# Copies of the identity moved from GpSimd to VectorE in an attention and feed-forward kernel, with a new order of all engines

## The chip, the cores and the metric

The kernel runs on one core of a Trainium2 chip. The time is device microseconds of one execution, and smaller is better. A core has a matrix engine (TensorE, PE in the profile), three engines for elementwise work (VectorE or DVE, ScalarE or ACT, GpSimd or POOL), a queue engine (SyncE or SP) and 16 DMA engines. Each engine takes its instructions in the order in which the program gives them, and an instruction that has to wait holds up everything behind it on its engine.

## The reference, cut to what matters

Attention with a decay over the keys, for 8 batches of 8 heads, 576 tokens and 64 columns a head, and behind it a feed-forward layer whose hidden values are the product of two projections:

```python
scores = scale * np.matmul(q, k.transpose(0, 1, 3, 2))
log_f = np.log(np.clip(f, 0.0001, 1.0))
cum = np.cumsum(log_f, axis=-1)
decay = cum[:, :, :, None] - cum[:, :, None, :]
scores = np.where(causal, -1000000000.0, scores + decay)
attn = softmax(scores)                       # over the keys
x = np.matmul(attn, v)                       # (8, 8, 576, 64), then as 4608 x 512
out = ((x @ w_a) * (x @ w_b)) @ w_out        # 512 -> 1536 -> 512
```

## The kernel before

**Tiles.** Two heads are worked on together as a pair (t = 0 to 31, four pairs per batch), one head on each half of the 128 partitions. The queries of a pair are cut into row blocks i = 0 to 4 of 128 (the last of 64), and a row block needs the keys up to itself. All matmuls take fp16 and add up in fp32.

**The stages of a pair.** q and k are loaded, made fp16 (by the DMA itself in batch 0, by POOL later: `cast_qk`), transposed on PE (`pe_transpose`, L359) and copied out of PSUM (`pe_evict`, L287 to L293). PE makes the scores (`qk_group`, L551). In batch 0 PE also adds the decay, by multiplying a row of cumulative sums (`crow`) with a one-hot column taken from `pick`, and the causal mask, by multiplying `low` with `neg64`. DVE takes the maximum (L646, later fused with the decay in L674), ACT the exponential with its sum (L705), DVE the reciprocal (L713 and L715), and POOL or ACT multiplies (`do_norm`: L726 on POOL, L724 on ACT). The result is transposed, on PE for the first pairs and by a DMA transpose later (PTA and PTB), multiplied with v (L769, L784), and copied into `xT`.

**The feed-forward layer** goes over 11 blocks of 256 to 512 tokens. Each has matmuls with w_a (`psa`) and with w_b (`psb`), all under L74, a copy on ACT, a product on DVE (L1073), matmuls with w_out (`pso`), a copy and a store. The first psa needs rows 0 to 255 of all four pairs of batch 0.

**The order.** The program is a table of 2353 steps (`Op`), each with a function that issues its instructions, an engine or a choice of engines, and the steps that it needs. Two strings that a planner wrote fix the rest: `ORDER` is one sequence of all steps, and each engine works through its own of them in that sequence; `CHOICE` has one letter for each step that may run on more than one engine (A for ACT, D for DVE, P for POOL, S for SP). `SLOTS` says which buffer of a ring each step takes. At the places where PE has nothing to do, 24 steps `wake` multiply the identity with itself, and nothing reads the result.

**The steps around the change.** `ident` (step 2, on POOL) writes the 128x128 identity `ident16`: a memset and a select. `pick` (step 3, L86 to L90) clears two tiles `pickh` and copies each of the four 32x32 diagonal blocks of the identity into `pick` and into one of `pickh`: two memsets and eight copies. `const` (step 4, L93 to L102, on POOL) makes `neg64` and two tiles `low`: three memsets and six selects. `flo` (L233) makes the low halves of `crow`, `clip` (L225), the logarithm (L260) and the scan (L228) its sums. The planner's table has 1.2 us for ident, 1.0 (DVE) or 2.1 (POOL) for pick and 2.2 for const. `CHOICE` sends pick to POOL.

```python
def picks(e):
    for x in pickh:
        VEC[e].memset(x, 0.0)
    for m in range(4):
        x = slice(32 * m, 32 * m + 32)
        VEC[e].tensor_copy(out=pick[x, :], in_=ident16[x, x])
        VEC[e].tensor_copy(out=pickh[m // 2][x, :], in_=ident16[x, x])
```

Of the kernel before, what the change touches and what calls it, by code (L numbers as in the profile page):

```python
# [25 lines left out]
def kernel(  # L26
# [13 lines left out]
    B, H, S, D = q.shape  # L40
# [64 lines left out]
    def paddings():  # L105
# [36 lines left out]
        PA:03212031203120312031203120312031;PB:01010101010101010101010101010101;S:010101101010100101011010101101  # L142
        00010110111101010101001011010110110011100101001101010101001010010101011001010010101010;a16:0210210212012
        01201201201201201210120210212012010201201201201202120120121021021021021021012021210120121021201202012;bc
        :0210210210210210210210210210;ff:03120312013203210320302302133030201230301201203211031120120320123012031
        20132103213212302102130230230132132013201231203023013231213201302310231023102103203203201321203120312030
        23023102132132321302130213213201320312012302310230232130230210321023123102310312301301203120312031203103
        21023120320320123102310203120120123023102302130230312031203123123102301230213023121320311032032103210310
        131023101230123120312032032102130213211321321332012301312301201203203203201;ht:0dcba981234567d0bc9a81324
        567d0bc9a813542d670cb9851a324d670bc19854a32d6708cb1a9543d2670c89b1a543d06279c8b51a3460dc2;n16:0110010100  # L150
        01010010101001010101;n32:0210202102101201201012012002020102101021210210;nv:01010101;osb:0101010110101010
        01010101101101010010;qd:010101010101010101010101;sc:0101010101010101101001010110101001100101010101101001
        0101101011010101011100101101010101101010010101010101010110110110101101010101;st:054321054321054321054321
        05432105
# [91 lines left out]
    o_k = Op(None, {"DVE": 1.0, "POOL": 2.1}, picks, [o_i], prio=-300, name="pick")  # L246
# [10 lines left out]
    for lo, hi in ((0, 256), (256, S)):  # L257
# [5 lines left out]
                prio=-300, name="fscan")  # L263
# [945 lines left out]
    for n in cuts:  # L1209
# [3 lines left out]
        0 1 46 52 2 58 5 6 29-31 37 32 33 38-40 34 36 35 42 62 3 47 53 4 43 267 262 500 7 8 54 48 41 9  # L1213
        56 50 44 10 82 59 60 83 11 85 91 97 61 86 87 92 12 45 66 287 71 55 49 51 63 64 57 93 288 98 289
        99 127 94 130 136 131 132 137 138 13 290 172 14 15 128 16 291 175 181 176 183 182 177 139 133
        142 96 339 268 141 135 263 17 279 274 173 18 67 144 143 184 65 88-90 187 145 178 217 220 226 264
        188-190 265 340 19 218 221 222 227 228 232 223 266 341 229 95 72 180 186 146 74 140 179 185 73
        134 230 192 191 225 224 75 20 21 113 22 233 234 269 84 103 109 270 114 271 231 104 105 110 203
        158 23 24 342 204 25 159 205 206 100 106 248 211 249 102 108 101 129 111 107 77 280 76 112 343
        212 148-150 166 26 167 121 256 117 27 28 154 122 257 115 155 281 174 151 156 235 283 193 199 153  # L1220
# [6 lines left out]
        409 415 416 294 252 213 209 253 316 317 210 214 318 1733 1734 319 403 365 323-325 258 215 216  # L1227
        259 320 360 284 286 285 247 308 273 326 1736 254 346 375 368 410 376 369 1741 404 443 444 1737
        1738 321 255 322 1742 353 327 370 445 502 377 378 503 1739 371 398 1735 512 332 495 1743 446 328
        504 417 372 420 421 427 428 447 329 1745-1747 330 422 331 1748 1744 379 366 373 418 374 352 513  # L1230
# [10 lines left out]
        1789-1791 1793 714 653 707 632 633 1792 706 598 600 626 625 619 614 1799 441 439 1794 596 442  # L1241
        1795 1797 562 721 584 547 534 561 715 654 708 592 578 722 585 440 599 1796 601 637 1798 627 620
        638 602 639 1774 709 723 719 577 621 611 591 604 597 603 729 724 1800 656 660-662 1809 1801 1811
# [8 lines left out]
        796 760 652 784 797 783 909 811 911 855 1862 1863 695 1864 771 901-903 755 696 905 761 769 762  # L1252
        1872 1873 1865 800 801 906 907 802 803 908 816 1874 814 812 743 735 910 912 779 742 794 818 798
        819 804 832 826 825 750 856 1876-1879 833 1875 820 827 828 821 1867 839 840 1868 1869 835 834
# [119 lines left out]
```

## Time and profile before

| | |
|---|---|
| runs | 400.53, 402.37, 403.38 us; median 402.37 |
| the profiled execution | 405.31 us, span 403.6 us from its first to its last instruction |
| granted TensorE clock, mean | 0.996 |
| PE busy by stretch (0 to 14, 14 to 40, 40 to 90 us) | 8.17, 23.51, 49.74 us |
| first feed-forward matmul (psa) | 40.1 us |
| DMA | 76.87 MB, 190 GB/s mean |

In a row of the order of time, the first number is the start in us from the first instruction, the second is how long the row lasts, then engine, line, operation, `out<-in` by the names of the tiles, shapes and the count of instructions that the row merges. In square brackets stands how long the engine was idle ahead of it, and what ended that. In the table of stretches, each engine has its busy us and, in brackets, its instructions. A grouped row has the count, the busy us and the mean ns of one instruction, and then the idle time before them and who ended it.

### The profile page before, as it was taken

To read this page: it belongs to the slowest core of one execution; us is meant where nothing else is said; L and a number is where in the kernel's file an instruction comes from. 1 tells how busy PE (TensorE), PEld (TensorE's weight loads), DVE (VectorE), ACT (ScalarE), POOL (GpSimd) and SP (SyncE) were. 2 spreads that over 40 slices of the span, in tenths; PEclk is the share of its full clock that TensorE was granted. 3 is DMA by queue.
4 is the path that set the end of the run, shared out by engine and by line. 5 is a ranking of instruction groups with operands and counts; after the bars stand their busy time and mean duration, and the time that the engine had idled before them with its cause. 6 is when DMAs were issued, how large, how long until landed. Compare 5 with 4: busy or idle time off the path is not lost.

```text
span 403.6 us, 14685 instructions
## 1 busy us (share of the span) xinstructions
PE 388.4 (96%) x5768; PEld 243.5 (60%) x5768; DVE 291.5 (72%) x958; ACT 288.1 (71%) x797; POOL 261.7 (65%) x485
## 2 busy tenths in 40 slices
PE   5798999999999999999999799999999999999997
PEld 2455887978867655555565455555555555556675
DVE  5687989998877899976978667778887673234141
ACT  4688899998897778767887688887968762423231
POOL 8699694977979489849988477788776583000000
PEclk9899999999999999999999999999999999999999
DMA  7989999999999999999989999999997787100112
GB/s 124 243 173 146 170 137 169 234 240 293 224 248 284 211 316 193 225 229 263 222 247 210 270 260 231 222 269 217 229 213 171 166 164 161 54 2 10 44 54 80
DMA packets 147365, 76.87 MB, mean 190 GB/s; under 512 B 124384, under 2 KB 128352, under 8 KB 147296
## 3 DMA queue, kind: packets, MB, share of 16 engines
q1 hardware_dynamic: 132856, 68.72, 74.4%
q0 software_dynamic: 14256, 7.08, 14.5%
q8 instruction: 45, 0.74, 0.7%
q14 instruction: 24, 0.20, 0.2%
q10 hardware_dynamic: 184, 0.14, 0.1%
HBM read 52.05 MB, written 9.58 MB: 153 GB/s over the span
## 4 chain that ended last, share of the span: by engine, by line
PE 74%; DMA 8%; POOL 8%; DVE 3%; issue 3%; ACT 2%; POOLq 0%; ACTq 0%; DVEq 0%
PE psb L74 20%; PE psa L74 20%; PE pso L74 17%; DMA PTB<-PB 5%; PE sc L551 4%; PE pvx L769 3%; POOL PA L726 3%; PE psT L359 2%; PE sc L539 2%; DVE S L674 2%; DMA q<-in_q_dram 2%; PE psP L74 1%; DMA out_dram<-osb 1%; PE sc L74 1%; POOL PB L726 1%
## 5 line engine op out<-in xcount | busy, mean ns | idle before, releaser
L674 DVE CUSTOM_DVE_ANT_0 S<-sc,spread 64x576 f32<-64x576 f32 (+4 forms) x232 | 125.8, 562 | 15.6 <-PE sc L551 2.6
L74 PE MATMUL psa<-xT,wa 128*64 128x512 f16 (+2 forms) x1056 | 113.7, 341 | 0.8 <-ACT a L289 0.5
L74 PE MATMUL psb<-xT,wb 128*64 128x512 f16 (+2 forms) x1056 | 113.3, 341 | 0.2 <-DVE ht L1073 0.2
L1073 DVE TENSOR_TENSOR ht<-psb,a 128x512 f16<-128x512 f32 (+1 forms) x114 | 73.5, 657 | 42.2 <-PE psb L74 27.1
L74 PE MATMUL pso<-wout,ht 128*64 128x512 f16 x840 | 101.9, 380 | 0.0
L726 POOL TENSOR_SCALAR PA<-PA,st 128x384 f16<-128x384 f16 (+2 forms) x188 | 87.6, 478 | 15.5 <-DVE st L715 9.4
L289 ACT CAST a<-psa 128x512 f16<-128x512 f32 (+1 forms) x114 | 63.0, 557 | 44.9 <-PE psa L74 41.1
L705 ACT ACTIVATE PA<-S,st 128x256 f16<-128x256 f32 (+2 forms) x168 | 84.0, 504 | 9.8 <-DVE st L674 8.7
L726 POOL TENSOR_SCALAR PB<-PB,st 128x512 f16<-128x512 f16 (+1 forms) x89 | 62.5, 709 | 26.4 <-DVE st L715 13.9
L74 PEld LDWEIGHTS <-wb 128*64 128x64 f16 x1056 | 58.9, 110 | 32.4 <-issue 2.2
L74 PEld LDWEIGHTS <-wa 128*64 128x64 f16 x1056 | 57.8, 110 | 33.1 <-issue 4.0
L74 PEld LDWEIGHTS <-ht 128*64 128x64 f16 x912 | 48.9, 110 | 34.4 <-issue 1.4
L705 ACT ACTIVATE PB<-S,st 128x512 f16<-128x512 f32 x56 | 40.3, 721 | 3.5 <-DVE st L674 3.4
L705 ACT ACTIVATION_READ_ACCUMULATOR PA<-S,st 128x1 f32 x168 | 32.2, 192 | 0.0
L701 ACT ACTIVATE PB<-S,st 128x576 f16<-128x576 f32 x28 | 21.7, 775 | 12.1 <-POOL PA L726 3.6
L674 DVE CUSTOM_DVE_ANT_1 S<-sc,spread 128x256 f32<-128x256 f32 x48 | 19.8, 420 | 9.9 <-POOL spread L631 2.7
L631 POOL TENSOR_SCALAR_AFFINE_SELECT spread<-spread 128x768 f32<-128x768 f32 x24 | 20.8, 867 | 7.6 <-DMA spread<-cum_d 7.6
L769 PEld LDWEIGHTS <-nv 128*64 128x64 f16 x640 | 22.5, 110 | 5.4 <-issue 0.5
L293 DVE COPY osb<-pso 128x512 f32<-128x512 f32 x17 | 11.7, 690 | 16.7 <-PE pso L74 11.6
L674 DVE DVE_READ_ACCUMULATOR2_ANT st<- 128x1 f32 (+1 forms) x280 | 23.0, 82 | 0.0
L715 DVE RECIPROCAL st<-st 128x2 f32<-128x2 f32 x128 | 17.9, 155 | 6.1 <-ACT PA L705 4.1
L291 POOL TENSOR_SCALAR q<-q 128x1152 f16<-128x1152 f32 x14 | 16.1, 1153 | 9.2 <-DMA q<-in_q_dram 3.5
(107 smaller groups left out, 492.2 us busy)
## 6 DMA issues: line engine op xcount, KB each, us to landing
spread<-cum_d SPq DMA_DIRECT2D x24, 576.0 KB, 6.4
out_dram<-osb SPq DMA_DIRECT2D x35, 256.0 KB, 3.3
q<-in_q_dram SPq DMA_DIRECT2D x14, 576.0 KB, 5.4
k<-in_k_dram SPq DMA_DIRECT2D x14, 576.0 KB, 5.4
v<-in_v_dram SPq DMA_DIRECT2D x24, 256.0 KB, 5.7
wout<-in_moe_w_out_dram POOLq DMA_DIRECT2D x3, 512.0 KB, 5.9
nv<-in_v_dram POOLq DMA_DIRECT2D x8, 128.0 KB, 4.8
wa<-in_moe_w_a_dram POOLq DMA_DIRECT2D x2, 512.0 KB, 7.2
```

What stands on the lines that cost most here:

```text
L74: nc.tensor.matmul(out=out[r], lhsT=lhsT[:, r], rhs=rhs, **kw)
L289: nc.scalar.copy(out=out_, in_=in_)
L291: VEC[e].tensor_scalar(out=out_, in0=in_, scalar1=0.125, scalar2=1.0, op0=MUL, op1=MUL)
L551: nc.tensor.matmul(out=dst, lhsT=lhsT, rhs=rhs, start=start, stop=stop, skip_group_check=True)
L631: nc.gpsimd.affine_select(out=c[:, :, 0:SM].rearrange("p h (j k) -> p h j k", k=128), in_=c[:, :, SM:2 * SM].rearrange("p h (j k) -> p h j ...
L674: nc.vector.tensor_tensor_reduce(out=o, in0=x, in1=y, scale=-1.0, scalar=3e38, op0=ADD, op1=MIN, accum_out=m)
L701: nc.scalar.activation(out=p_blocks(t, 4), in_=T[("s" if direct else "z", t, 4)], func=EXP, bias=st[:, 8:9], scale=sign, accum_out=st[:, 1 ...
L705: nc.scalar.activation(out=p_blocks(t, i)[:, :, h, :], in_=(T[("s", t, i)][:, h, :] if direct else T[("z", t, i)][:, h * n:h * n + n]).rea ...
L715: nc.vector.reciprocal(out=st[:, 20 + 2 * i:22 + 2 * i], in_=st[:, 10 + 2 * i:12 + 2 * i])
L726: VEC[e].tensor_scalar(out=p, in0=p, scalar1=st[:, c:c + 1], scalar2=1.0, op0=MUL, op1=MUL)
L769: nc.tensor.matmul(out=o[HP[h], 128 * i:128 * i + 128], lhsT=vt[:, j, pr + NP * h, :], rhs=pt[:, base_blk[i] + 2 * block_at(t, i, j) + h, ...
L1073: nc.vector.tensor_tensor(out=ht[:, 0:n_], in0=T.pop(("psb", t0, fbs))[:, 0:n_], in1=T.pop(("a16", t0, fbs))[:, 0:n_], op=MUL)
```

## The change

One line of the table fixes `pick` on DVE. The three strings `ORDER`, `CHOICE` and `SLOTS` are replaced as a whole; the functions, the instructions of each step and the feed-forward blocks stay.

```diff
-    o_k = Op(None, {"DVE": 1.0, "POOL": 2.1}, picks, [o_i], prio=-300, name="pick")
+    o_k = Op("DVE", 1.0, picks, [o_i], prio=-300, name="pick")
...
     ORDER = """
-        0 1 46 52 2 58 5 6 29-31 37 32 33 38-40 34 36 35 42 62 3 47 53 4 43 267 262 500 7 8 54 48 41 9
-        56 50 44 10 82 59 60 83 11 85 91 97 61 86 87 92 12 45 66 287 71 55 49 51 63 64 57 93 288 98 289
...
+        0-2 52 46 62 58 5 6 29 3 30 31 37 32 38 33 39 34 36 40 35 42 4 47 53 43 262 500 267 7-9 48 54 10
+        44 56 50 41 82 63 83 11 85 91 65 86 87 97 64 12 49 51 55 13 59 45 57 66 67 74 88 89 287 99 98 92
...
     CHOICE = """
-        ASPDDPDADAAADDDPPPPPAPAPAAADPPPPPPPAPDADDPPPPPPPPADDDDPPPPPPAPPADAADDAAAADDADPPPPPPPAPAADAPA
+        SADDPDADDADADAPPPAPPPPPDDADAPPAPPAPPDDDDPAPAAPPPPDADDAPAPPAAAPDAAADADAAAADDDAPPPPPPPAADDAPAP
...
```

Sorted by engine, the new strings put these steps first (k0 and q1 stand for the halves of k and q of batch 0, m for a second part of a load):

| engine | before | after |
|---|---|---|
| POOL | load k0, load q0, **ident**, load k1, load q1, **pick**, load k0m, load q0m, **const**, flo, paddings, load v | **ident**, load q0, load k0, load q1, load k1, **const**, load k0m, load q0m, flo, paddings, load v |
| DVE | memsets, clip, clip, scan, scan, copy and flo of crow, maxima | memsets, **pick**, clip, clip, scan, scan, copy and flo of crow, maxima |
| ACT | logarithms, copies to qT and kT, table for the exponential | logarithms, table for the exponential, copies to qT and kT |
| PE | 4 wakes, transposes q0, k0, 2 wakes, scores of pair 0 | 5 wakes, transposes k0, q0, 1 wake, scores of pair 0 |
| SP | load f, store of sums, loads q, k of batch 1, q of batch 2 | load f, store of sums, loads k of batch 1, q of batch 2, q of batch 1 |

Of the steps with a choice, 20 normalizations go from POOL to ACT and 7 from ACT to POOL, all in pairs 0 to 7; some 60 copies out of PSUM change between ACT and DVE over the whole kernel. The matmul steps that stand ahead of the first psa are the same but for one (`ptr1A1` in place of `ptr0A1`), and all 24 wakes still stand among them.

More of the change, by code (lines that the diff above doesn't have):

```diff
@@ L147 @@
[L147 to L151, printed above, removed]
@@ L152 @@
[L152 to L154 removed]
+        PA:03212310230123012301230123012301;PB:01010101010101010101010101010101;S:010110101001011010101010101101
+        00101010100101010101001010110101010101010101101010101100101010110101001010101010101010;a16:0210210210210
+        21021021021021021201201201201201201201201201201021012012012012021021021021212021010210210210120120120;bc
@@ new lines @@
+        :0210210210210210210210210210;ff:03120312021321302312013202022000102102301321302302101231023013223013021
+        32031021321320313010312031230231023012310231031231203121320312012031230123010231203120120312031201301031
+        20310231023123102102121321012102103213021301231201302312010230130231031010310230132012301203120321032013
+        01201302310230213210310230132102103120312012120320321321023103201320132013213023102120302132032103210321
+        023012130130132130213230130132013201301301301303012301203120320320320320321;ht:0dcba981234567d0bc9a18234
@@ L155 @@
+        567d0bc89a154320d769bc8451ad203769b5c481ad203794b65ac81d2036974cb5a81d24306c97b51a83d4206;n16:0110101010
+        01101101010101010101;n32:0210101212021021021210101020212010210102121001;nv:01010101;osb:0101010101010010
+        00101101010101001010;qd:010101010101010101010101;sc:0110101010101010101010100101010101010011101100100101
+        0101010101010101010011010100100101111010101001001011011010010100101010101010;st:054321053421053421053412
+        05341205
     """
@@ new lines @@
+        44 56 50 41 82 63 83 11 85 91 65 86 87 97 64 12 49 51 55 13 59 45 57 66 67 74 88 89 287 99 98 92
+        93 61 60 263 268 127 130 136 172 288 14-16 131 138 137 132 128 289 175 181 176 142 182 177 183
+        139 178 133 184 279 274 264 17 290 291 173 18 143 144 217 179 71 140 185 135 339 180 186 203 19
+        187 220 226 188 189 100 145 190 204 218 232 147 77 221 228 227 222 340 20-22 94 229 265 341 269
[11 rows of a table added]
+        320 321 259 322 326 368 369 327 1738 260 261 370 1741-1743 216 376 1739 377 1744 446 502 398
[15 rows of a table added]
@@ new lines @@
+        642 1820 643 641 720 729 622 715 578 724 679 591 680-682 1824 1826 645 644 646 561 1804 563 585
[4 rows of a table added]
+        1847 756 757 774 758 1849 759 1850 811 651 1851 782 775 754 788 760 734 1852 789 748 1853-1855
+        781 1848 1856 1857 711 712 776 652 790 791 713 1858 772 777 783 784 693 694 1808 1859 901 695
+        1862 923 904 911 855 795 812 762 761 742 735 750 755 736 796 743 769 696 902 785 903 797 771 814
+        1863 1864 787 817 749 905 912 792 800 818 798 801-803 820 1872 826 825 819 1860 832 778 821 828
@@ new lines @@
+        1873 827 1865 816 1874 1867 1876 833 1875 815 906 839 829 840 804 907 861 806 799 856 779 813
+        780 805 831 931 763 764 1861 1868 834 1877 835 841 1878 1879 908 909 1869 1880-1882 1884 1883
[3 rows of a table added]
+        1898-1900 928 859 932 1902 940 933 946 934 1901 880 939 947 1903 1904 850 857 838 881 874 1107
[11 rows of a table added]
+        1088 1090 1091 1075 967 1964-1966 968 1963 1967 1968 1130 1970 1093 1048 1969 1134 1136 1092
[4 rows of a table added]
+        1987 1132 1120 1155 1145 1152 1196 1156 1122 1129 1160 1988-1991 1121 1161 1053 1054 1098 1097
[10 rows of a table added]
@@ new lines @@
+        2039 1340 1357 1358 2007 1315 1373 2048 2045 2049 1345 1211 1256 1327 1213 1263 1322-1324 1271
[6 rows of a table added]
+        1426 1427 1507 2073 1508 1509 1432-1434 1438 1435 2076 2077 2074 2078 2080 1422 2082 1439 1441
+        2081 2084 2086 1341 1349 1405 1467 1400 1399 1392 2079 1384 1326 1385 1445 1410 1446 2085 1447
+        1440 2083 1421 1464 1419 1462 1412 1411 1393 1386 1428 1468 2087 1475 1469 1482 2088 2090 1470
+        2089 2092 1477 2093 1471 2091 1442 1369 1531 1529 1517 1414 2075 2070 1483 1476 1478 2094-2096
[8 rows of a table added]
@@ new lines @@
+        1620 1563 1568 1570 1663 2133 1524 1579 1549 2136-2138 1527 2139 1503 1526 1608 1609 1525 1611
+        1622 1610 1626 1627 1544 1587 1504 2140 1625 1669 1664 1612 1640 1634 1633 1600 1613 1628 1636
+        1635 1629 2141 2144-2146 2148 1641 2149 1643 1637 2142 1630 2147 1666 1606 1670 2150 1671-1673
[4 rows of a table added]
+        1530 1653 1696 1654 1655 1697 1656 1650 1676 1639 1675 1659 2143 2180-2182 2184 1694 1698 1699
+        2185 2183 1700 2175 1573 1617 2186 2188 2190 2192 2193 1574 2189 2191 1657 1658 1651 1660 2187
@@ L1323 @@
+        1618 2194 2197-2199 1661 2202 2195 2200 1702 1695 1701 1689 1690 1683 1704 1703 2203 2204 2207
[4 rows of a table added]
+        2289 2268 2270-2272 2275 2276 2269 2264 2291 2273 2277 2292-2295 2278 2296 2298 2297 2299-2301
+        2274 2279 2328 2302-2308 2310 2312 2309 2314 2313 2311 2315 2316 2318 2320 2317 2321 2319
+        2322-2324 2326 2325 2327 2329-2335 2338-2340 2343-2345 2336 2337 2341 2346 2342 2347-2352
     """
     CHOICE = """
-        ASPDDPDADAAADDDPPPPPAPAPAAADPPPPPPPAPDADDPPPPPPPPADDDDPPPPPPAPPADAADDAAAADDADPPPPPPPAPAADAPA
@@ L1326 @@
-        PAPPPPPADADPPPPPPPAADADAPPPAPPPPPADAADDDADAADADAAAAAAAAAADAAADDADDDDADAADDADAAAADAAAAAAAAAAA
-        ADADDDADADADDAAAAAADDDDDAADDDDDAAADAAADAADDADAADAD
+        SADDPDADADDADAPPPAPPPPPDDADAPPAPPAPPDDDDPAPAAPPPPDADDAPAPPAAAPDAAADADAAAADDDAPPPPPPPAADDAPAP
+        APPPPPDAADPAAPPAPPPDAAAAPPAAAPPADADAAAADDADAAADAAADAAAAADADDADDADADADDAAAADAAAADDAAAADDDAAAA
+        AADDADADDAADDAADAAAADAAAADAADDAAADAADADDAAADADADD
     """
```

38 lines of the change are left out of this document (removed), and 155 rows, old and new, of the table ORDER.

## The prediction

> **What bounds the kernel now.** I read the page first, then five stretches of the span, then the chain of waits of the first 41 us, then the first 16 us in order of time.
>
> ```profile
> span 403.6 us, 14685 instructions
> ...
> PE 388.4 (96%) x5768; PEld 243.5 (60%) x5768; DVE 291.5 (72%) x958; ACT 288.1 (71%) x797; POOL 261.7 (65%) x485
> ```
> ```profile
> core 0: us, PE busy (x) PEld busy (x) DVE busy (x) ACT busy (x) POOL busy (x), PEclk, DMA share, GB/s
> 0.00:14.00 14.00, 8.17 (x128) 4.00 (x128) 7.88 (x16) 6.93 (x15) 12.12 (x41) 1.00 0.86 174
> 14.00:40.00 26.00, 23.51 (x436) 14.29 (x436) 19.55 (x45) 21.28 (x66) 22.02 (x40) 0.93 0.94 170
> 40.00:90.00 50.00, 49.74 (x1040) 40.58 (x1036) 46.44 (x162) 48.22 (x132) 37.30 (x61) 1.00 1.21 193
> 90.00:345.00 255.00, 251.23 (x3568) 150.55 (x3566) 200.95 (x710) 195.56 (x556) 190.24 (x345) 1.00 1.02 228
> ```
> PE is busy 49.74 of the 50 us from 40 to 90 and 251.23 of the 255 after that, so from 40 to 345 us it stands still for 0.26 + 3.77 us in all. The first 40 us are different: their 8.17 + 23.51 busy us hold the 24 `wake` steps, which compute nothing. So the start of the first feed-forward matmul (psa) is the mark to watch. If it comes earlier, a nearly full PE moves with it. The chain of waits says who is late ahead of the mark (columns: start, us, what):
>
> ```profile
> 8.17 6.31 DMA q<-in_q_dram
> ...
> 20.92 0.02 POOL PA L726
> ...
> 28.89 0.59 POOL wb L510
> 29.48 0.04 issue
> 29.52 2.85 POOL PA L726 x6
> ...
> 40.15 0.88 PE psa L74 x13
> ```
> First comes a load that POOL issued at 8.17 and that landed at 14.48; later POOL itself, from 20.92 to 32.4, with normalizations (L726), casts and the issues of weight loads. Now the start, first POOL's rows alone, then those of the other engines:
>
> ```profile
> 1.33 0.81 POOL L334 DMA_DIRECT2D k<-in_k_dram  x1 [0.81 <-POOLq L1358]
> ...
> 2.73 0.22 POOL masks.py:197 MEMSET ident<- 128x128 f16 x1
> 3.03 0.29 POOL masks.py:199 TENSOR_SCALAR_AFFINE_SELECT ident<-ident 128x128 f16<-128x128 f16 x1
> ...
> 4.72 0.21 POOL L86 MEMSET pick<- 128x32 f16 x2
> ...
> 6.20 0.79 POOL L89 COPY pick<-ident 32x32 f16<-32x32 f16 x1
> ...
> 7.37 0.27 POOL L90 COPY pick<-ident 32x32 f16<-32x32 f16 x1
> 7.58 0.60 POOL L334 DMA_DIRECT2D k<-in_k_dram  x1
> 8.17 0.60 POOL L334 DMA_DIRECT2D q<-in_q_dram  x1
> 8.81 0.15 POOL L93 MEMSET neg<- 128x64 f16 x1
> ...
> 10.28 0.54 POOL L102 TENSOR_SCALAR_AFFINE_SELECT low<-low 64x128 f16<-64x128 f16 x2
> ```
> ```profile
> 3.37 3.34 PE L74 MATMUL wake<-ident 128*64 128x512 f16 x16 [3.37 <-POOL ident masks.py:199]
> ...
> 4.42 0.70 DVE L225 TENSOR_SCALAR cum_f<-cum_f 96x256 f32<-96x256 f32 x2 [2.16 <-DMA cum_f<-in_f_dram]
> ...
> 4.87 0.78 ACT L260 ACTIVATE cum_l<-cum_f 96x256 f32<-96x256 f32 x2 [1.25 <-DVE cum_f L225]
> ...
> 5.32 1.67 DVE L228 TENSOR_TENSOR_SCAN cum_f<-cum_f,cum_l 96x256 f32<-96x256 f16 x2 [0.21 <-ACT cum_l L260]
> ...
> 7.16 0.65 ACT L287 ACTIVATE qT<-psT 128x576 f16<-128x576 f16 x1 [1.51 <-PE psT L359]
> ...
> 8.36 1.28 ACT L221 ACT_TABLE_LOAD   x1
> ...
> 8.55 0.34 PE L551 MATMUL sc<-crow,pick 64*128 64x256 f16 x4
> ...
> 10.63 0.51 PE L551 MATMUL sc<-neg,low 64*128 64x64 f16 x7 [0.59 <-POOL low L102]
> ...
> 11.17 1.96 DVE L646 TENSOR_REDUCE st<-sc 128x2 f32<-128x512 f32 x3 [2.21 <-PE sc L551]
> ...
> 14.53 0.47 PE L359 MATMUL psT<-ident,q 64*64 64x64 f16 x18 [1.41 <-DMA q<-in_q_dram]
> ...
> 16.14 0.34 PE L551 MATMUL sc<-kT,qT 64*128 64x256 f16 x4
> ```
> pick holds POOL from 4.72 to 7.64, 2.92 us for two memsets and eight copies. Behind it stand two loads and the mask constants, which end at 10.82. The first scores have their decay from `pick` by 8.89 and then wait for the masks (low); the last mask matmuls end at 11.14, and DVE's first maximum follows at 11.17.
>
> **The change, part by part.**
>
> *pick on DVE.* In the new list it stands behind DVE's first memsets and ahead of the clip of f, where DVE is idle for 2.16 us (row of 4.42). No row shows such a copy on DVE; I bound it by two small instructions of that engine:
>
> ```profile
> 0.88 0.06 DVE L216 MEMSET warm<- 128x1 f32 x1 [0.88 <-PEq L1358]
> ```
> ```profile
> 16.78 0.17 DVE L715 RECIPROCAL st<-st 128x2 f32<-128x2 f32 x1
> ```
> Ten of them are 0.6 to 1.7 us; the ends stay, and I take 1.0, nearer to the memset, because two of the ten are memsets and the copies are 32 elements wide. The idle time covers all of it, provided `ident` is there in time, so it costs nothing. Without that cover (ident at 3.32, as now) the clip would come at 4.3 to 5.0 instead of 4.42, up to 0.6 late, and all that hangs on the scan with it.
>
> *POOL's new start.* ident (2.73 to 3.32: 0.59) now goes first: 1.33 to 1.92. Four loads of batch 0 follow; two of them took 1.33 to 2.73 and two 3.32 to 4.72, 2.8 together, so they end at 4.7. Then the constants (8.81 to 10.82: 2.0) to 6.7, and then the two loads of 7.58 and 8.17, now at 6.7 and 7.3. One thing speaks against: a pick copy took 0.79 us where the last took 0.27, and it ended at 6.99 just as DVE's two scans did (5.32 + 1.67). Now the constants lie beside the scans. If their six selects are held as that copy was, twice (once for each scan), they lose 2 × 0.52 = 1.0 us: 7.7 and 8.3. So the second load gains between 0.9 us and minus 0.1. I take 0.6, nearer to the unhindered end, because the memsets of the constants come first. The Trainium skill, page "SBUF — State Buffer", section "Who interferes with whom", gives a reason for that row: a DVE instruction with two SBUF inputs contends with a GpSimd instruction that reads SBUF, though not with one that only writes. The row agrees with it; the sum by the rule in full would use the minus 0.1.
>
> The first loads of q and k are issued up to 0.6 us later, behind ident. Their transposes now wait behind wakes (3.37 + 3.34 = 6.71); the wakes start 1.4 us earlier. The cost is between nothing and 0.6; I take nothing, as ACT sets the next step: it loads its exponential table ahead of qT in the new list, from 5.65 (4.87 + 0.78) for 1.28 and a short instruction, until about 7.1, and qT began at 7.16.
>
> *First scores.* The masks are ready at 6.7 to 7.7, before the scores. The mask matmuls follow those of pick directly: 8.9 + about 0.3 = 9.2 instead of 11.14. DVE's first maximum gains 1.9 us.
>
> *Pair 1.* The second load lands 0.6 earlier, at 13.9; transposes (0.47) and a copy (0.75 on DVE now) give its scores at 15.2 instead of 16.14: 0.9, with 0.2 to 1.2 as ends.
>
> ```profile
> 16.00 0.75 DVE L291 TENSOR_SCALAR qT<-psT 128x576 f16<-128x576 f16 x1
> ```
> *Normalizations from POOL to ACT.* Counted along the two lists, 20 of them go to ACT and 7 come back, all of batches 0 and 1: 13 net, 6 by the trace's 40 us and 7 in the stretch to 90.
>
> ```profile
> L726 POOL TENSOR_SCALAR PA<-PA,st 128x256 f16<-128x256 f16 (+2 forms) x44 | 20.6, 478 | 11.1 <-DVE st L715 9.4 <-ACT PB L705 1.3
> ```
> At 0.48 us each POOL loses 2.9 us of work ahead of the mark and 3.4 after it. POOL's stretch from 20.92 to 32.4, which is the chain today, shrinks by about 2.9. What is late next is DVE: 19.55 busy us in the 26 from 14 on, and it gets three evictions more (3 × 0.75), with the last copy of batch 0 into xT behind them all. For psa I take a gain of 2.3: its ends are pair 1's 0.9, if DVE holds all that follows, and 2.9 + 0.6 = 3.5, if POOL stays the chain; it lies nearer to POOL, which the chain names. So psa starts at 37.8 instead of 40.1.
>
> *From 40 to 90 us* ACT is busy 48.22 of 50 and gets 7 × 0.48 = 3.4 us more. Its idle 1.8 doesn't hold that; 1.6 is left over, against a stage that starts 2.3 earlier. I take a loss of 0.5, with 0 and 1.6 as ends.
>
> *After 90 us* evictions swap between ACT and DVE (23 go to ACT, 20 to DVE), and the changes between shapes of matmul on PE stay (212 in the old list, 211 in the new). No row gives this a sign: I cost it at nothing. What hides it is PE's full queue; if that cover is gone at the transfers, which the new order meets elsewhere, the price is that of the 3.77 us above once more: between a gain of half of it (1.9) and a loss of all of it (3.8).
>
> **The sum.** −2.3 + 0.5 = −1.8 us. The profiled execution's own 405.31 (its span 403.6 and 1.7 around it) becomes 403.5, with a span of 401.8. It was 2.9 above the median of the runs shown (402.37, of 400.53 to 403.38), so I set the 1.8 against that median: 400.6.
>
> **The rivals.**
> 1. *The gain is hidden.* Batch 0 is through earlier, but the rows of batch 1 come no sooner, because DVE and ACT are 93% and 96% busy from 40 to 90 and can't use the earlier start; PE then runs out of batch 0 and waits. For it: those shares. Against it: POOL, not these two, is the chain before the mark. Time: 402.4, between 401.5 and 404.
> 2. *Slower: ACT becomes the bound of 14 to 90.* It does 21.28 + 48.22 = 69.5 us of work in those 76, 91%; 13 × 0.48 = 6.2 more makes 75.7. Started 1.9 earlier it has 78, so it must be 97% full to be done at 90 as now: above that share the change gains, below it loses. At 91% it needs 82.8 and ends 4.8 late: 402.37 + 4.8 = 407.2. For it: no stretch before shows ACT above 96%. Against it: part of ACT's idle time before 40 is waiting for maxima, which come earlier.
> 3. *More goes than the start.* psa gains 3.1, and half of the 3.77 us goes too: 402.37 − 3.1 − 1.9 = 397.4. For it: those waits are few and large. Against it: nothing in the diff aims at them.
> 4. *The copies on DVE hold up POOL's issues.* They now lie beside POOL's first loads. If they stop the writing of descriptors, the first q and k come later by pick's 0.6 to 1.7, past what the wakes and ACT's table cover, and the gain at the first scores falls to some 0.8: about 401.8. For it: the copy of 0.79 shows that DVE can hold POOL. Against it: issues beside DVE memsets took no longer than 0.81. The Trainium skill, the same page, section "SBUF: two separate sides", describes this as a trap for DMAs from the GpSimd queue beside DVE copies in its faster modes; no row of before shows it.
>
> **How the numbers follow.** A measurement of this kernel tells a change of about 1% from none: the bounds are 398.35 and 406.39. The forecast (398.4 to 402.0) has 0.42, rival 1 0.22, rival 2 0.17, rival 3 0.12, rival 4 0.07. Faster by over 1%: rival 3 and a little of the forecast's edge, 0.15. Slower by over 1%: most of rival 2, 0.13, and 0.03 for the loss of 3.8 after 90 on top of rival 1: 0.16. Within 1%: 0.69. The range runs from rival 3's 397.4 towards rival 2's 407.2, drawn in a little at each end so that two in ten stay out: 397.8 to 406.5.
>
> **What would show it.** Right: POOL starts with ident at 1.3; pick on DVE is over before f lands; the first mask matmuls wait for nothing; DVE's first maximum comes at about 9.3; the two loads of pair 1 are issued at 6.7 to 8.3; psa starts at about 37.8; PE stays above 49 of 50 us from 40 to 90 with ACT at 49 or more. Wrong: the clip later than 4.5, or the load of pair 1 landing after 14.5, breaks the start; PE idle for over 1 us between 38 and 90 behind ACT breaks the step from 40 to 90; new waits of PE for DMA transposes after 90 break what I put at nothing.

## The result and the profile after

The change makes no difference that can be measured. The kernel after takes 402.64 us (median of 22 runs, 400.14 to 404.81), the kernel before 402.86 us (22 runs beside it, 400.53 to 409.12); the ratio is 1.000, 95% interval 0.9978 to 1.0023. Here and below a ratio pairs a kernel with the kernel before on the same chip and leaves disturbed runs out, so it need not be the quotient of two medians. The profiled execution of after took 402.58 us with a span of 400.8 us. That of before (405.31) was 2.45 us above its median, so the two spans by themselves say too much.

The stretches of the kernel after, in the columns used for before:

```profile
core 0: us, PE busy (x) PEld busy (x) DVE busy (x) ACT busy (x) POOL busy (x), PEclk, DMA share, GB/s
0.00:14.00 14.00, 8.87 (x146) 4.45 (x146) 9.54 (x26) 8.54 (x21) 12.76 (x34) 1.00 0.84 174
14.00:40.00 26.00, 23.21 (x406) 14.14 (x404) 19.86 (x44) 18.59 (x62) 16.47 (x29) 0.87 0.95 168
40.00:90.00 50.00, 49.88 (x1042) 40.58 (x1036) 45.53 (x155) 48.88 (x135) 35.60 (x56) 1.00 1.16 187
90.00:345.00 255.00, 254.82 (x3611) 152.44 (x3607) 200.46 (x715) 201.06 (x568) 190.01 (x345) 1.00 1.01 230
```
POOL has lost a quarter of its work from 14 to 40 us (16.47 busy us, 22.02 before). But ACT and DVE have not filled up there (18.59 and 19.86), and the granted clock of PE is 0.87 where it was 0.93. Something comes later than planned. The order of time of the kernel after shows it; these rows answer to those of the start before:

```profile
2.31 0.07 DVE L86 MEMSET pick<- 128x16 uint32 x1
...
3.32 0.35 DVE L90 COPY pick<-ident 32x32 f16<-32x32 f16 x1
...
3.92 0.94 DVE L225 TENSOR_SCALAR cum_f<-cum_f 96x256 f32<-96x256 f32 x2 [0.26 <-DMA cum_f<-in_f_dram]
...
4.36 0.21 POOL L93 MEMSET neg<- 128x64 f16 x1
...
5.16 0.92 POOL L102 TENSOR_SCALAR_AFFINE_SELECT low<-low 64x128 f16<-64x128 f16 x2
...
6.15 0.65 POOL L97 TENSOR_SCALAR_AFFINE_SELECT neg<-neg 64x64 f16<-64x64 f16 x1
...
6.75 0.81 POOL L102 TENSOR_SCALAR_AFFINE_SELECT low<-low 64x128 f16<-64x128 f16 x2
...
7.07 0.65 ACT L287 ACTIVATE qT<-psT 128x576 f16<-128x576 f16 x1 [0.18 <-PE psT L359]
...
8.11 0.60 POOL L334 DMA_DIRECT2D q<-in_q_dram  x1
...
8.96 2.04 DVE L646 TENSOR_REDUCE st<-sc 128x2 f32<-128x512 f32 x3 [0.26 <-PE sc L551]
...
13.59 0.47 PE L359 MATMUL psT<-ident,k 64*64 64x64 f16 x18 [2.59 <-DMA k<-in_k_dram]
...
16.20 0.69 PE L359 MATMUL psT<-ident,q 64*64 64x64 f16 x18 [2.15 <-DMA q<-in_q_dram]
16.82 1.07 PE L74 MATMUL wake<-ident 128*64 128x512 f16 x4
...
18.44 0.50 PE L551 MATMUL sc<-kT,qT 64*128 64x256 f16 x4
```
The first half of the plan is there: pick ends on DVE at 3.67, before f lands, and DVE's first maximum comes at 8.96 instead of 11.17. Then PE waits twice for the loads of pair 1, 2.59 and 2.15 us, and the scores of pair 1 begin at 18.44 instead of 16.14. The chain of waits of the kernel after goes through the same load, and to the same mark as before:

```profile
8.11 8.05 DMA q<-in_q_dram
...
41.20 0.99 PE psa L74 x16
```
(The chain's row of psa starts 0.07 us behind the first psa matmul, which is the mark in the text and the tables.) A second profile of the kernel before (run e0 below) shows how far one profile can be trusted. Its chain of waits:

```profile
8.66 7.49 DMA q<-in_q_dram
...
42.22 1.00 PE psa L74 x16
```
The same program had the load at 16.14 (14.48 in the first profile) and psa at 42.15 (40.08). A second profile of after (e10) had the load at 15.72 and psa at 40.28 (16.16 and 41.13). So psa came on average 0.4 us earlier (40.7 against 41.1), where 2.3 were forecast. With 2.1 us between two profiles of one program this is no measurement of the difference; it agrees with the medians.

### The profile page after: what moved, and what is told of

It is laid out like the page before. It is cut to its first block, busy times and chain, and to the rows that moved or that the text cites. A ratio compares the mean times of both kernels' runs of the same rounds, so it can differ in the third digit from the quotient of the medians.

```text
span 400.8 us, 14675 instructions
## 1 busy us (share of the span) xinstructions
PE 389.7 (97%) x5768; PEld 249.9 (62%) x5768; DVE 293.1 (73%) x968; ACT 291.5 (73%) x810; POOL 254.9 (64%) x462
## 4 chain that ended last, share of the span: by engine, by line
PE 91%; DVE 3%; DMA 3%; ACT 2%; POOL 1%; issue 0%; DVEq 0%; ACTq 0%
PE psb L74 23%; PE psa L74 23%; PE pso L74 22%; PE sc L551 5%; PE pvx L769 3%; PE psT L359 2%; PE sc L539 2%; DMA q<-in_q_dram 2%; PE psP L74 2%; PE wake L74 2%; PE sc L74 2%; PE pv L769 1%; PE pvx L784 1%; DVE S L674 1%; DMA cum_f<-in_f_dram 1%; ACT PA L705 1%
## 5 line engine op out<-in xcount | busy, mean ns | idle before, releaser
L1073 DVE TENSOR_TENSOR ht<-psb,a 128x512 f16<-128x512 f32 (+1 forms) x114 | 74.4, 658 | 53.7 <-PE psb L74 42.3
L726 POOL TENSOR_SCALAR PA<-PA,st 128x128 f16<-128x128 f16 (+2 forms) x173 | 81.0, 478 | 20.8 <-DVE st L715 16.9
L726 POOL TENSOR_SCALAR PB<-PB,st 128x512 f16<-128x512 f16 (+1 forms) x91 | 63.8, 707 | 27.3 <-DVE st L715 13.4
L74 PEld LDWEIGHTS <-wa 128*64 128x64 f16 x1056 | 60.7, 110 | 30.1 <-issue 1.8
L74 PEld LDWEIGHTS <-wb 128*64 128x64 f16 x1056 | 60.4, 110 | 29.9 <-issue 1.8
L74 PEld LDWEIGHTS <-ht 128*64 128x64 f16 x912 | 50.0, 110 | 33.3 <-issue 2.4
L769 PEld LDWEIGHTS <-nv 128*64 128x64 f16 x640 | 21.9, 110 | 4.8 <-issue 0.2
L289 ACT COPY osb<-pso 128x512 f32<-128x512 f32 x22 | 12.8, 582 | 14.3 <-PE pso L74 13.8
L701 ACT ACTIVATE PB<-S,st 128x576 f16<-128x576 f32 x28 | 21.6, 773 | 1.6 <-issue 1.1
L551 PE MATMUL sc<-kT,qT 64*128 64x512 f16 (+4 forms) x144 | 21.3, 332 | 1.0 <-ACT kT L289 0.7
L638 POOL TENSOR_SCALAR_AFFINE_SELECT spread<-spread 128x256 f32<-128x256 f32 x24 | 9.7, 404 | 19.1 <-DVE st L674 19.0
```

Source lines behind the costliest of these rows:

```text
L74: nc.tensor.matmul(out=out[r], lhsT=lhsT[:, r], rhs=rhs, **kw)
L289: nc.scalar.copy(out=out_, in_=in_)
L551: nc.tensor.matmul(out=dst, lhsT=lhsT, rhs=rhs, start=start, stop=stop, skip_group_check=True)
L638: nc.gpsimd.affine_select(out=x, in_=x, compare_op=mybir.AluOpType.is_ge, fill=NEGBIG, base=0, pattern=[[0, 2], [-1, 128]], channel_multip ...
L701: nc.scalar.activation(out=p_blocks(t, 4), in_=T[("s" if direct else "z", t, 4)], func=EXP, bias=st[:, 8:9], scale=sign, accum_out=st[:, 1 ...
L726: VEC[e].tensor_scalar(out=p, in0=p, scalar1=st[:, c:c + 1], scalar2=1.0, op0=MUL, op1=MUL)
```

## The experiments

The theory at the outset was that the whole gain hangs on one load: POOL's load of the second half of q for pair 1 (step 53, issued behind step 47). The new order puts the constants (step 4) ahead of both, they are slowed beside DVE's scans, and so the load is not issued earlier. The rivals were that SP's three loads of 576 KB (steps 262, 500, 267) take the bandwidth, that the wakes are in the way, and that the other engines in their new shares set the pace. All runs in one table (us; "landed" is step 53; "psa − scores" is from the first scores of pair 1 to psa; times of one profiled execution each, except median and ratio):

| run | issued → landed | scores of pair 1 | psa | psa − scores | median (runs) | ratio to before, 95% |
|---|---|---|---|---|---|---|
| before | 8.17 → 14.48 | 16.14 | 40.08 | 23.9 | 402.86 (22) | |
| e0 before again | 8.66 → 16.14 | 18.34 | 42.15 | 23.8 | one run, 404.72 | |
| e3 pick alone | 5.31 → 11.11 | 13.83 | 37.35 | 23.5 | 400.56 (12) | 0.9934 (0.9899–0.9969) |
| e11 e3, constants first | 8.43 → 14.68 | 16.34 | 40.17 | 23.8 | 401.99 (10) | 0.9975 (0.994–1.0011) |
| after | 8.11 → 16.16 | 18.44 | 41.13 | 22.7 | 402.64 (22) | 1.000 (0.9978–1.0023) |
| e10 after again | 8.11 → 15.72 | 18.00 | 40.28 | 22.3 | one run, 401.53 | |
| e1 loads first | 4.95 → 12.96 | 14.36 | 36.91 | 22.6 | 399.20 (6) | 0.9892 (0.9848–0.9936) |
| e2 bulk later | 8.01 → 16.44 | 18.72 | 40.64 | 21.9 | 402.57 (12) | 0.9978 (0.9945–1.001) |
| e5 both | 4.96 → 13.87 | 15.28 | 36.92 | 21.6 | 399.48 (7) | 0.9923 (0.9894–0.9951) |
| e6 constants early | 6.92 → 14.13 | 16.30 | 38.22 | 21.9 | 401.45 (10) | 0.9979 (0.9955–1.0004) |
| e9 bulk from ACT | 8.12 → 12.80 | 14.21 | 36.64 | 22.4 | 401.69 (10) | 0.9926 (0.9879–0.9972) |
| e4 pick back | 10.49 → 17.82 | 20.10 | 42.37 | 22.3 | 405.59 (7) | 1.0095 (1.0064–1.0127) |
| e7 fewer wakes | 4.96 → 14.18 | 15.59 | 37.23 | 21.6 | 400.53 (12) | 0.9944 (0.9914–0.9975) |
| e8 normalizations back | 4.95 → 12.50 | 13.90 | 42.97 | 29.1 | 408.58 (4) | 1.0152 (1.0112–1.0192) |

From psa to the end of the span the profiles show 359.5 to 362.3 us in all runs but before's first profile (363.5) and e8 (364.9), in the old order (e0 360.9, e3 359.8, e11 360.0) as in the new. So within 2.9 us the time follows psa, and the column "psa − scores" splits psa in two: when pair 1 can begin, and how long the rest of batch 0 then takes.

**Before and after again** (e0, e10): no edit.

> The kernel before, unchanged, to see in a second profile whether its first 40 us and its later waits were typical. Theory (the new order starts its first psa 1.1 us later, 41.1 against 40.1, and the profile of before happened to have more waits later): psa again at 39.5 to 40.5, and PE idle from 40 to 345 us by 1 to 3 us instead of the 4.0 of the first profile; span 399.5 to 402.5. Rival (the old order always has those waits, and the new order really removed them): PE idle by 3.5 to 4.5 us again, span 402.5 to 404.5.

> The changed kernel, unchanged, for a second profile. Expected: the load of pair 1 issued at 8.0 to 8.3 and landed at 15.5 to 17, psa at 40.5 to 42, PE idle from 40 to 345 us by 0.3 to 2; span 400 to 402.5. If psa came below 39.5, the first profile's late load would not be typical, and the account of the lost gain would fall.

Measured: the rows of the table. psa moves by 2.1 us between two executions of before and by 0.9 between two of after. e0 missed its expectation for psa (42.15 for 39.5 to 40.5) and for the span (403.0 us for at most 402.5); PE's idle time from 40 to 345 us, 1.8 us, lies inside it. A difference of 1 us in a single profile carries no verdict here.

**Loads first** (e1): the two loads of pair 1 ahead of the constants, in the new order.

```diff
-... 36 40 35 42 4 47 53 43 262 500 267 ...
+... 36 40 35 42 47 53 4 43 262 500 267 ...
```


> The changed kernel with the two loads of pair 1 (steps 47 and 53) put ahead of the mask constants on POOL. Theory (these loads, issued at 8.1 us behind constants that DVE's scans stretched, and landing at 16.2 beside SP's loads, took the start's gain back): issued at 4.4 and 5.0, landed by 11.5; the scores of pair 1 at 13 to 15 instead of 18.4; constants end at about 8.7, so the first masks wait by 0 to 0.4; psa at 38 to 39 instead of 41.1; time 1.5 to 2.5 us below the changed kernel, 400.1 to 401.1, ratio to before 0.993 to 0.996. Rival (the chain to psa is DVE and the wakes at half clock, whatever the load does): psa at 40.3 or later, time within 0.6 of 402.6.

Measured: 399.20 us, ratio 0.9892 (0.9848 to 0.9936): faster than both kernels, by 4.4 us (1.1%) in the ratio. From its order of time:

```profile
4.95 0.63 POOL L334 DMA_DIRECT2D q<-in_q_dram  x1
...
7.80 1.05 POOL L102 TENSOR_SCALAR_AFFINE_SELECT low<-low 64x128 f16<-64x128 f16 x2
...
13.00 0.47 PE L359 MATMUL psT<-ident,q 64*64 64x64 f16 x18 [0.76 <-DMA q<-in_q_dram]
13.40 0.62 PE L74 MATMUL wake<-ident 128*64 128x512 f16 x4
...
14.36 0.34 PE L551 MATMUL sc<-kT,qT 64*128 64x256 f16 x4
```
The load is issued 3.16 us earlier than in after and lands 3.20 earlier. It took 8.01 us all the same, so it landed at 12.96 and not by 11.5 as expected. The masks end 1.3 us later (8.85 for 7.56), and the first maximum comes only 0.24 us later (9.20 for 8.96). One place in POOL's list was worth 1.1%.

**Bulk later** (e2): SP's load of q of batch 2 (step 500) behind a later one, so that two loads of 576 KB lie beside pair 1's instead of three. The buffer numbers of one ring (n32) change with it.

```diff
-... 262 500 267 7-9 ... 279 274 264 ...
+... 262 267 7-9 ... 279 274 500 264 ...
```


> The changed kernel with SP's load of q of batch 2 (step 500, 576 KB, needed after 40 us) put behind the loads of batch 1, so that it is issued at about 21 us instead of 8.1. Theory of contention (the load of pair 1 took 8.05 us because three loads of 576 KB lay beside it): it lands at 13.5 to 14.5 instead of 16.2, psa at 39 to 40, time 0.8 to 1.8 below the changed kernel. Rival (POOL's queue lands late for itself, whatever SP moves): landing at 15.7 or later, psa above 40.6, time within 0.5 of 402.6.

Measured: the load took 8.43 us (8.05 in after), 402.57 us, ratio 0.9978 (0.9945 to 1.001). The gain from the third load gone did not come, and the landing at 16.44 is what the rival expected; e9 decides between the two. The DMA share from 8 to 14 us is 1.08 in e2 and 1.06 in after, so two such loads fill the engines as three do.

**Bulk from ACT** (e9): all three loads of 576 KB are issued by ACT, behind its exponentials of pair 0.

```diff
-... 43 262 500 267 7-9 ... 92 93 61 ...
+... 43 7-9 ... 92 93 262 500 267 61 ...
...
-        nc.sync.dma_start(out=x.rearrange("p j t d -> p j (t d)"), in_=src)
+        late = (which, b, half) in (("k", 1, 0), ("q", 2, 0), ("q", 1, 0))
+        (nc.scalar if late else nc.sync).dma_start(out=x.rearrange("p j t d -> p j (t d)"), in_=src)
```


> The changed kernel with the three loads of 576 KB (k and q of batch 1, q of batch 2) issued by ACT behind its exponentials of pair 0, at about 13 us, instead of by SP at 7.7 to 9.2; POOL's queue stays, with the constants ahead of the loads of pair 1. Theory (POOL's loads land late because SP's packets of 2304 bytes take two thirds of the DMA engines from 8 us on): the loads of pair 1, issued at 8.1 as before, land at 10.5 to 13 instead of 16.2, the scores of pair 1 at 13 to 15 instead of 18.4, clock 1.00; the bulk loads land at 17 to 20, about where POOL takes them up now; psa at 37.5 to 39.5. Rival (POOL's loads are slow by themselves): landing at 15 or later.

Measured: ratio 0.9926 (0.9879 to 0.9972), with single runs from 397.58 to 405.2. The load was issued as in after (8.12) and took 4.68 us. The DMA view of the time between, first of the kernel after (8.7 to 13.5 us), then of e9 (8.7 to 11 us); q0 is POOL's queue, q1 SP's; the columns are packets, MB, and the share of the 16 engines:

```profile
q1 hardware_dynamic: 464, 0.97, 61.8%
q0 software_dynamic: 323, 0.34, 43.6%
```
```profile
q0 software_dynamic: 300, 0.31, 93.1%
q1 hardware_dynamic: 57, 0.08, 9.9%
```
POOL's queue moved 0.34 MB in 4.8 us beside SP's loads (71 GB/s) and 0.31 MB in 2.3 us without them (135 GB/s). So sharing the DMA engines is a second cause of the late load, and with it gone psa comes at 36.64 although the constants still stand ahead. (The granted clock, expected at 1.00, was 0.93 from 14 to 40 us.)

**Both** (e5): the edits of e1 and e2 together, the ring's included.

> The kernel with the loads of pair 1 ahead of the constants, and besides that SP's load of q of batch 2 behind the loads of batch 1. In the former POOL stood at 19.7 us with its cast of q of batch 1 (step 268), whose load was the third of SP's and landed at 19.54. Theory (after pair 1's loads, that wait is next on the way to psa): the load lands at 16.5 to 17.5, the cast starts then, the first normalization of pair 2 (step 179) at 18 instead of 20.8, psa at 34.5 to 36 instead of 36.9, time 397.2 to 398.6. Rival (DVE, full from 14 us on, is next, and POOL's wait lies beside it): psa at 36.5 or later and time within 0.5 of 399.2.

Measured: psa 36.92 and 399.48 us, ratio 0.9923 (0.9894 to 0.9951): the same as e1 within the intervals. That fits e2.

**Constants early** (e6): step 4 behind POOL's second load, ahead of the third and fourth, where DVE does not scan yet.

```diff
-        0-2 52 46 62 58 5 6 ... 42 4 47 53 43 ...
+        0-2 52 46 4 62 58 5 6 ... 42 47 53 43 ...
```


> The changed kernel with the mask constants put ahead of two of POOL's four first loads, so that they run at about 2.9 us, before DVE's scans (5.0 to 6.8) but beside pick's copies on DVE; the loads of pair 1 follow two loads behind. The constants took 3.20 us in the changed kernel and 2.01 before. Theory of the port (selects on POOL stand while DVE reads two inputs): they take 2.0 to 2.5 us here, ended by 5.4, and the loads of pair 1 are issued at 6.7 and 7.3 instead of 7.5 and 8.1, landed at 13 to 15.5; psa at 39.5 to 41. Rival (POOL is slow there because it still writes the descriptors of loads that it issued): 3 us or more again, and the loads of pair 1 no earlier than 7.5.

Measured: the constants took 2.02 us (2.91 to 4.93), as in before (2.01), and not 3.2:

```profile
2.91 0.18 POOL L93 MEMSET neg<- 128x64 f16 x1
...
4.30 0.63 POOL L102 TENSOR_SCALAR_AFFINE_SELECT low<-low 64x128 f16<-64x128 f16 x2
...
4.72 1.73 DVE L228 TENSOR_TENSOR_SCAN cum_f<-cum_f,cum_l 96x256 f32<-96x256 f16 x2 [0.19 <-ACT cum_l L260]
```
They lie beside pick's copies on DVE and end as the scan begins. Two loads stand right ahead of them here too, so the rival, that POOL is slow behind loads that it has just issued, falls. The load is issued 1.19 us earlier, psa comes at 38.22 (39.5 to 41 was expected), and the ratio is 0.9979 (0.9955 to 1.0004): between after and e1 in the profile, not distinct from no change in time.

**Pick alone** (e3): the kernel before, with pick on DVE and nothing else.

```diff
-    o_k = Op(None, {"DVE": 1.0, "POOL": 2.1}, picks, [o_i], prio=-300, name="pick")
+    o_k = Op("DVE", 1.0, picks, [o_i], prio=-300, name="pick")
...
-        0 1 46 52 2 58 5 6 29-31 37 ... 42 62 3 47 53 4 43 ...
+        0 1 46 52 2 58 5 6 29 3 30 31 37 ... 42 62 47 53 4 43 ...
```


> The kernel before with one part of the change alone: pick on DVE, between its first memsets and the clip, in the old order. ident is ready at 3.3 there, so pick lies at 3.4 to 4.6 and may push the clip by up to 0.6. Theory (what the copies cost on POOL is worth about 2 us when the loads of pair 1 move up with them): the loads at 4.7 and 5.3 instead of 7.6 and 8.2, landed by 11.5; constants end at about 8.5 instead of 10.8; psa at 37.5 to 38.5 instead of 40.1; time 400.3 to 401.3, ratio 0.993 to 0.997. Rival (POOL's normalizations from 21 to 33 us are the chain and are not moved by an earlier start): psa at 39.5 or later, time within 0.5 of 402.9.

Measured: 400.56 us, ratio 0.9934 (0.9899 to 0.9969). pick alone in the old order brings 0.7%, more than the whole change. Against e1 (0.9892) the intervals overlap, so the runs do not show in the time what the rest of the new order is worth. From its order of time and its chain of waits:

```profile
5.31 0.62 POOL L334 DMA_DIRECT2D q<-in_q_dram  x1
```
```profile
37.42 0.99 PE psa L74 x16
```

**Pick alone, constants first** (e11): e3 with the new order's place of the constants.

```diff
-        ... 42 62 47 53 4 43 ...
+        ... 42 62 4 47 53 43 ...
```


> The old order with pick on DVE, and one step moved as the new order has it: the constants ahead of the loads of pair 1 on POOL. With pick on DVE alone, psa came at 37.35 and the time was 400.56. Theory (that place of the constants is what costs the new order its gain): the constants at 4.7 to 7.9, the loads of pair 1 issued at 7.9 and 8.5 and landed at 14.5 to 16.5 instead of 11.1, psa at 39.5 to 41.5, time 402 to 403.5. Rival (the rest of the new order is at fault): psa below 38.3, time within 0.7 of 400.6.

Measured: 401.99 us, ratio 0.9975 (0.994 to 1.0011). Its chain of waits:

```profile
8.43 6.25 DMA q<-in_q_dram
...
40.24 0.99 PE psa L74 x16
```
The load is issued 3.12 us later than in e3, about where it was in before (8.43 for 8.17), and psa is where it was in before: in the profile this place alone takes back what pick on DVE brought. It is e1 in reverse, in the other order. The times point the same way but do not settle it: the interval of e11 holds no change and overlaps that of e3.

**Pick back** (e4): the new order with pick on POOL, behind the first four loads.

```diff
-        0-2 52 46 62 58 5 6 29 3 30 31 37 ...
+        0-2 52 46 62 58 3 5 6 29-31 37 ...
```


> The changed kernel with one part undone: pick runs on POOL again, behind the four loads and ahead of the constants, in the new order. Theory (the place of POOL's loads of pair 1 in its queue sets the start): pick 4.4 to 7.3, constants to 9.6, the loads of pair 1 at 9.6 and 10.2 and landed at 16.5 to 18; first maximum at about 10; psa at 42 to 43.5 instead of 41.1; time 0.8 to 2 us above the changed kernel, 403.4 to 404.6. Rival (the first 15 us have enough slack): psa within 0.5 of 41.1, time as the changed kernel's.

Measured: 405.59 us (403.4 to 404.6 was expected), ratio 1.0095 (1.0064 to 1.0127). pick takes POOL from 4.35 to 7.68, and the load of pair 1 is issued at 10.49. In the new order, with the constants ahead of the loads, pick on DVE is needed to stay level with before.

**Fewer wakes** (e7): e1, and the last 10 of the 24 wakes issue nothing.

```diff
-        o = Op("PE", 0.427, lambda _: wake(2), [o_i], ...
+        o = Op("PE", 0.427, lambda _, n=n: wake(2) if n < 14 else wake(0), [o_i], ...
```


> The kernel with the loads of pair 1 ahead of the constants, and the last 10 of the 24 wakes issue nothing (their results are read by nobody). In that kernel the chain from 23 us to psa is PE itself, and wakes stand on it: 0.43 + 0.45 + 0.64 + 0.62 + 0.56 + 0.60 + 0.59 + 0.87 = 4.8 us. Theory (they are now in the way): psa at 34.5 to 36 instead of 36.9, clock 1.00 all the same, time 397 to 398.6. Rival (PE would wait for DVE and POOL in their places): psa at 36.4 or later, time within 0.5 of 399.3; or the granted clock falls in 14 to 40 us and psa comes later.

Measured: 400.53 us, ratio 0.9944 (0.9914 to 0.9975), no better than e1. The stretch of e7 from 14 to 40 us, and its chain of waits:

```profile
14.00:40.00 26.00, 20.02 (x440) 14.11 (x442) 22.77 (x50) 22.83 (x72) 19.54 (x35) 1.00 1.10 194
```
```profile
24.68 0.60 POOL wb L510
25.31 2.41 POOL PA L726 x5
27.72 0.60 POOL wb L510
```
The wakes stand in the chain of after and e1, but only as fillers: without ten of them PE is 3.6 us less busy than in e1 (20.02 for 23.66), the chain goes through POOL instead, and psa is not earlier (37.23). It comes 21.6 us behind the scores, 0.9 less than in e1, but e5 with all its wakes has 21.6 too.

**Normalizations back** (e8): e1, with the 27 exchanged normalizations on their old engines (20 to POOL, 7 to ACT), in the new order.

```diff
-        SADDPDADADDADAPPPAPPPPPDDADAPPAPPAPPDDDDPAPAAPPPPDADDAPAPPAAAPDAAADADAAAADDDAPPPPPPPAADDAPAP
+        SADDPDADADDADAPPPPPAPAPDDADPPPPPPPAPDDDDPPPPPPPPADADDPPPPPPAPPDAAADADAAAADDDPPPPPPPAPADDAPAP
...
```


> The kernel with the loads of pair 1 ahead of the constants, and the 27 normalizations back on the engines that they had before (20 to POOL, 7 to ACT), in the new order. Theory (POOL is the chain from 20 to 30 us, so the normalizations that ACT took are worth some 2 us): psa at 38 to 40 instead of 36.9, POOL busy at over 24 of the 26 us from 14 to 40, time 400 to 402. Rival (the start's gain comes from the loads alone, and the exchange between POOL and ACT is worth nothing): psa within 0.7 of 36.9, time within 0.6 of 399.2.

Measured: 408.58 us, ratio 1.0152 (1.0112 to 1.0192); psa is 29.1 us behind the scores of pair 1. The stretch of e8 from 14 to 40 us:

```profile
14.00:40.00 26.00, 18.90 (x292) 10.66 (x292) 17.46 (x39) 17.30 (x55) 18.82 (x35) 0.93 1.03 175
```
POOL, expected to be busy for over 24 us, is less busy than in e1 (18.82 for 19.84), so the loss is not POOL's added work but waits: from 14 to 43 us POOL itself waits 5.1 us for DVE's reciprocals (L713) and 3.2 for a load of q, and PE (psP) 3.6 for POOL's PA. An order made for one assignment stalled with another here. The run does not say what the exchange was worth in the old order, and that was not tried.

## Why the prediction was right and wrong

That the time would stay within 1% came true. The gain of 1.8 us (0.45%) did not come: the interval of the ratio allows 0.9 us at most, and 402.64 lies outside the forecast's own 398.4 to 402.0. The step that failed is the start of pair 1. At the mark its loss cancels most of what the rest of the order brought, and that the two would cancel was not foreseen. Step by step:

- **pick on DVE: right.** It ran from 2.31 to 3.67, 1.36 us where 1.0 was taken (0.6 to 1.7 as ends), inside the idle time, and the clip came at 3.92.
- **First loads behind ident, and the first maximum: right.** qT began at 7.07 (forecast 7.1), the maximum at 8.96 (forecast 9.2).
- **POOL's new start: inside its ends, at the bad one.** POOL's four loads ended at 4.36, but the constants took 3.20 us. Their selects lost 1.07 us against before: the rows 0.92, 0.65 and 0.81 stand against 0.53, 0.24 and 0.54. That is the full price of 1.0 which the prediction had worked out from the held pick copy and then set at 0.3. The load of pair 1 was issued at 8.11, a gain of 0.06 where 0.6 was taken.
- **Pair 1: here the prediction failed.** "The second load lands 0.6 earlier, at 13.9": it landed at 16.16, 2.3 us later than that. Of this 0.54 is the issue. The other 1.74 is the transfer, costed at the 6.31 us of one profile, and it took 8.05. It is no constant: with three loads of 576 KB beside it, it took 6.31 and 7.49 in the two executions of before, 8.05 and 7.61 in those of after, and 4.68 without them (e9). Issued at 4.95 or 4.96 in the new order with all three, it took 8.01, 7.55 and 9.22 (e1, e8, e7). Behind it came another 1.0 us, from landing to scores 2.28 us where 1.3 was forecast; the rows of before had 1.66 (16.14 less 14.48), so the forecast was short here too. After its waits PE ran slowly: four wakes took 1.07 us at 16.82, where e1 has them in 0.62 at 13.40 and needs 1.40 us from landing to scores. So the scores of pair 1 came at 18.44 instead of 15.2. The prediction itself named "the load of pair 1 landing after 14.5" as what would break the start.
- **Normalizations: the size came, its cause is not shown.** The prediction put 1.4 us of psa's 2.3 on what follows pair 1's scores (2.3 less 0.9). From scores to psa the old order takes 23.5 to 23.9 us in four runs, the new one 21.6 to 22.7 in nine (all but e8): 1.6 us less between the means. POOL's normalizations ahead of 40 us fell by 3.3 us (forecast 2.9), and by 2.6 counted up to psa itself, as after has one more of 0.7 us between 40 us and its psa; in the groups of the first 40 us, before and then after:

```profile
L726 POOL TENSOR_SCALAR PA<-PA,st 128x128 f16<-128x128 f16 (+2 forms) x21 | 9.4, 459 | 3.6 <-DVE st L715 3.5
...
L726 POOL TENSOR_SCALAR PB<-PB,st 128x512 f16<-128x512 f16 (+1 forms) x3 | 2.1, 707 | 0.3 <-DVE st L715 0.2
```
```profile
L726 POOL TENSOR_SCALAR PA<-PA,st 128x256 f16<-128x256 f16 (+2 forms) x13 | 6.1, 477 | 8.4 <-DVE st L715 8.3
...
L726 POOL TENSOR_SCALAR PB<-PB,st 128x512 f16<-128x512 f16 (+1 forms) x3 | 2.1, 703 | 0.6 <-DVE st L715 0.3 <-DVE st L713 0.2
```
  That these 1.6 us are the exchange and not another part of the new order is argued from those rows; e8 could not show it alone, and some of the nine runs have further edits.
- **psa: −2.3 forecast, −0.4 measured** over two profiles each: pair 1's scores are 1.0 later (18.2 against 17.2) instead of 0.9 earlier, and the rest is 1.4 shorter in these four profiles.
- **From 40 to 90 us: the loss of 0.5 did not come.** PE is busy 49.88 of 50 and ACT 48.88.
- **After 90 us: nothing, as costed.** PE lost only 0.18 us there, where before's first profile lost 3.77; but e0 has 1.38, e3 0.68 and e11 1.29, and e3 and e11 in the old order need as long from psa to the end as the new order does. Most of those 3.77 us belonged to one execution.

Of the rivals, the first (hidden from 40 to 90) came within 0.3 us of the time with the wrong mechanism: PE does not wait there, and where psa came early, as in e1, the end came early too. The second fell because ACT, at 48.88 of 50, held nobody up: PE was busy for 49.88 there. The third fell because the start did not gain. For the fourth no sign was seen: POOL's four issues beside and behind pick took 0.80, 0.60, 0.74 and 0.73 us, those before 0.81, 0.60, 0.74 and 0.72.

## What to carry to other kernels

Freeing an engine helps when the instruction that the chain waits for moves up in its queue. Look at who stands ahead of it in the new order: here 3.2 us of constants took the place of 2.9 us of pick, and putting two loads ahead of the constants gave 1.1%. A transfer's time from one profile is the time beside the transfers of that execution; before it is used as a constant, a second profile or the other queue's issues should bound it. Two profiles of the unchanged kernel differed by 2.1 us at the mark, nearly the 2.3 that the change was to bring.

## What the hardware showed that was not expected

GpSimd's selects beside two-input instructions of VectorE (the scans, L228, and the sums of crow, L233) made the whole step about 1.6 times as long: the constants took 3.20 us in after and 3.32 in e1, against 2.01 in before, where VectorE was idle beside nearly all of them (the 2.21 us ahead of the first maximum), and 2.02 in e6, where they ended 0.2 us into the scan. The Trainium skill, page "SBUF — State Buffer", section "Who interferes with whom", says that a VectorE instruction with two SBUF inputs contends with a GpSimd instruction that reads SBUF, and one with a single input, outside its faster modes, does not. The four runs agree on the first half, and the prediction should have used the full price; on the second, e6's constants lost nothing beside pick's copies (pick itself took 1.59 us there, 1.36 in after), and which mode those copies ran in no run shows. Who pays can differ: in e3 the constants took only 2.43 us beside the scans, but the scans 2.14 where before has 1.67.

In the DMA view of after, POOL's queue got 0.34 of 1.31 MB, 26%, while SP's loads were in flight. The Trainium skill, page "DMA: Bandwidth & Descriptors", section "Queues, rings and completion order", says that a DMA engine goes round its queues packet by packet. If the packets that the profile counts are those, the trace agrees in kind: POOL has 323 of 787 packets, 41%, but its packets average 1.05 KB (0.34 MB in 323) and SP's 2.1 KB (0.97 MB in 464), so the queue with the smaller packets gets a still smaller share of the bytes.

After PE's waits of 2.59 and 2.15 us for pair 1, its granted clock in after is 0.50 from 16 to 22 us. In e1, with waits of 0.61 and 0.76 us, and in e3, with none, it is 1.00 there. In that sense the late load was paid for twice, by the wait and by slower matmuls behind it. That the waits lower the clock is argued from this comparison, since no run changed them alone. The runs give no rule for how long a wait must be: with one wait each, of 1.41, 2.58 and 3.07 us, the clock from 16 to 22 us is 0.72 in before, 0.50 in e0 and 0.72 in e11.
